# Another hand-written order on every engine, and 70 matmuls on a zero tile in the ramp

## The chip, the cores and the metric

One core of one Trainium2 chip. A core has TensorE (PE, with its weight loads shown as PEld), VectorE (DVE), ScalarE (ACT), GpSimd (POOL), SyncE (SP, which here only issues transfers) and 16 DMA engines. The metric is the device time of one execution in microseconds (us).

## The reference

Causal attention over q, k, v of shape (4 batches, 8 heads, 768 positions, 64), followed by a gated two-layer network over all 3072 rows:

```
scores = q @ k^T / 8
heads 0, 2, 6 (retrieval): keep keys at or before the query
heads 1, 3, 4, 5, 7 (stream): of these keep keys 0..3 and the last 64
a = softmax(scores);  x = a @ v, heads side by side: (3072, 512)
h = x @ w_in                 w_in (512, 2048)
g = h * sigmoid(beta * h)
out = g @ w_out              w_out (2048, 512), out in float32
```

## The kernel before

The work is cut into 8 chunks of 384 rows (half of a batch's positions; the first halves of batches 0 and 1 are chunks 0 and 1) and each chunk into 4 units of two heads. A unit's attention is: cast q and k to bf16, transpose them on PE, copy the transposes out of PSUM (`copy_qk`, L330 for k, L333 for q), multiply to scores (L451, `sp` banks), exp on ACT (L460), multiply with v (L520, `po` banks or a third kind, `mm`), divide by the sum on DVE (`normalize`, L529 and L533). Masks are added in PSUM by matmuls with an identity (L422) in the first 8 units, except unit 5; elsewhere DVE multiplies them onto the exps. Sink positions have copies of their own: `KO` for keys (L312), `VO` for v (L259, L260). Two units' results are transposed to `xT` (L558, copied at L567). From units 12 on q and k come as rows by GpSimd transfers (`load_rows`, L282) and are transposed by DMA.

The network follows per chunk: 16 groups of the first product (`steps_G1`, 4 matmuls of 128x384, L588), each with a tanh on ACT (L593) and a gate on DVE (L596); then, for each 128 rows, 4 groups of 4 matmuls of 128x512 of the second product (`steps_G2`, L641), a copy out on ACT (L645) and a store from SP.

There is no scheduler: each engine runs its instructions in the order in which the program emits them. That order is written out by hand, word by word. `RAMP` covers units 0 to 7 and the whole first product of chunks 0 and 1; `PLAN` has one line for each further unit; `TAIL` feeds what is left. `do` (L685 and after) reads a word: `ck`/`cq` cast k or q of a unit, the last letter being the engine (v DVE, a ACT, g POOL); `tk`/`tq` transpose, `kk`/`kq` copy the transpose out; `ad`, `qk`, `ex`, `ma` are the masks in PSUM, scores, exps and DVE masks of one tile of a unit; `pv` two of the six steps of the product with v; `no` normalize; `ko`, `vo` sink copies; `cv` cast a v tile; `lq`, `lv` load a chunk's q and k or a v tile by SP; `wi`, `wo` load a quarter of w_in or w_out by POOL; `ro` one transfer of rows by POOL; `xx`, `cx` transpose x and copy it out; `hm`, `hf` the first and second half of a first-product group, `mm`, `mA` a whole one (`mA` in an `sp` bank), `mb` a second-product group; `on` ones beside v; `ne`, `ml` masks; `be` beta; `tt` both transposes of a unit; `dk`, `dq` the DMA transposes of rows. In `PLAN`, `V` is a step of scores, `p` of the product with v, `a`/`A` and `b` groups of the two products, `T` and `X` transposes.

Ahead of the ramp, `idle(8, ps_m, "mm")` (L167) runs eight 128x512 matmuls on `zeros`, a bf16 tile of 128x512, while the first transfers are on their way.

PSUM has two `sp` tiles of two banks, three `mm` banks and one `po` bank. Stage tiles for q and k (`s0`, `s1`) and for v (`vs`) have two buffers each.

Of the kernel before, what the change touches and what calls it, by code (L numbers as in the profile page):

```python
# [10 lines left out]
F32 = mybir.dt.float32  # L11
# [7 lines left out]
def kernel(  # L19
# [13 lines left out]
    nc = tc.nc  # L33
    B, H, S, D = q.shape
# [467 lines left out]

    def steps_PV(u):
# [3 lines left out]
        def head(hh, qi, last):  # L507
            def go():
                for f in s["masks"] + chunk_values[u // NPAIR] if u >= 8 else []:
                    f()  # L510
                if "po" not in s:
                    if u < 8 and u % 2:
                        po = ps_m.tile([128, 512], F32, name="mm")
                        s["po"] = po[:, 0:HT * 2 * (D + 1)].rearrange("p (t h d) -> p t h d", t=HT, h=2)
                    else:
                        s["po"] = ps_o.tile([128, HT, 2, D + 1], F32, name="po")
# [168 lines left out]
    def do(word):  # L685
# [70 lines left out]
    def feed(x):  # L756
# [27 lines left out]
        mA mm ro3 mA mm ro3 mm mm ro3 mA mA mb mb tt8 mb mb mb
# [3 lines left out]
    for word in words:  # L788
# [27 lines left out]
        b a A p a p a a b a A p p A b a p b a p
        b A X a A b A
# [42 lines left out]
    i = 0  # L860
# [39 lines left out]
```

## Time and profile before

| | us |
|---|---|
| three runs | 228.45, 229.58, 230.4 (median 229.58) |
| the profiled execution | 231.07 |
| its span, first to last instruction | 229.1 |

The profile is of one execution. Spans and durations below are its own; the 1.97 us between the span and the execution's time lie around the span. A row of the timeline gives start, duration, engine (with a q for an issue by its queue), line, operation, output<-inputs, shape, count, and in brackets the idle time of that engine just before and what ended it.

### The profile page before, as it was taken

How to read it: one execution, taken by the hardware profiler on the slowest of the kernel's cores; microseconds unless marked ns; L12 is line 12 of the kernel's file. 1: busy time of each engine (PE TensorE's matmuls, PEld its weight loads, DVE VectorE, ACT ScalarE, POOL GpSimd, SP SyncE). 2: the span in 40 equal slices, each digit the busy share in tenths (PEclk: the TensorE clock that was granted, in tenths of full speed). 3: DMA queues.
4: the chain of work that ended last, by engine and by line, in shares of the span. 5: the costliest groups of instructions: out<-in, count | busy, mean ns of one | idle time of the engine just before them, and what ended most of it. 6: DMA issues, size and time to landing. Idle time of an engine off the chain costs nothing.

```text
span 229.1 us, 5018 instructions
## 1 busy us (share of the span) xinstructions
PE 223.1 (97%) x1907; PEld 127.4 (56%) x1907; DVE 141.8 (62%) x342; ACT 154.3 (67%) x254; POOL 87.6 (38%) x143
## 2 busy tenths in 40 slices
PE   7899999999999999999999999999999999999994
PEld 2456666654565665555654565455654656455553
DVE  4458988875286588536952588546963779028600
ACT  2567988864868799438944697759876878138621
POOL 5373991219636269535028038940560000000000
PEclk9999999999999999999999999999999999999999
DMA  6999999999999999969778969496983130111012
GB/s 202 262 297 247 215 197 203 232 193 161 196 142 97 181 164 156 122 173 156 111 149 109 158 132 173 86 163 93 194 70 83 47 83 0 49 46 46 0 49 92
DMA packets 95383, 31.66 MB, mean 138 GB/s; under 512 B 81776, under 2 KB 92416, under 8 KB 95360
## 3 DMA queue, kind: packets, MB, share of 16 engines
q1 hardware_dynamic: 58880, 22.82, 48.6%
q0 software_dynamic: 35904, 8.13, 39.8%
q10 hardware_dynamic: 576, 0.40, 0.5%
q8 instruction: 15, 0.25, 0.4%
q14 instruction: 8, 0.07, 0.1%
HBM read 27.27 MB, written 6.29 MB: 146 GB/s over the span
## 4 chain that ended last, share of the span: by engine, by line
PE 94%; DMA 2%; ACT 1%; SPq 0%; issue 0%; ACTq 0%
PE mm L641 35%; PE mm L588 25%; PE sp L588 12%; PE sp L451 8%; PE po L520 7%; PE mm L322 2%; DMA s<-in_k_dram 2%; PE sp L422 2%; PE mm L626 2%; PE mm L558 1%; PE mm L520 1%; PE mm L451 1%; ACT qkb L246 1%; SPq L119 0%; ACT es L460 0%; ACT KT L330 0%
## 5 line engine op out<-in xcount | busy, mean ns | idle before, releaser
L641 PE MATMUL mm<-w_out_sb,gT 128*128 128x512 bf16 x368 | 85.9, 379 | 0.0
L460 ACT ACTIVATE es<-sp 128x768 bf16<-128x768 f32 (+2 forms) x72 | 56.6, 837 | 21.4 <-PE sp L451 21.2
L588 PE MATMUL mm<-xT,w_in_sb 128*128 128x384 bf16 x348 | 64.6, 326 | 0.0
L588 PEld LDWEIGHTS <-w_in_sb 128*128 128x128 bf16 x512 | 47.8, 98 | 29.8 <-issue 0.2
L593 ACT ACTIVATE th<-mm,beta_h 128x384 f32<-128x384 f32 x87 | 49.7, 587 | 5.7 <-PE mm L588 0.9
L641 PEld LDWEIGHTS <-gT 128*128 128x128 bf16 x368 | 33.4, 98 | 36.0 <-issue 1.5
L596 DVE SCALAR_TENSOR_TENSOR gT<-th,mm 128x384 bf16<-128x384 f32 x87 | 46.7, 551 | 6.7 <-ACT th L593 3.2
L282 POOL DMA_DIRECT2D s<-in_q_dram x30 | 22.4, 763 | 26.3 <-DMA QTD<-s 19.8
L588 PE MATMUL sp<-xT,w_in_sb 128*128 128x384 bf16 x164 | 32.3, 326 | 0.0
L645 ACT ACTIVATE osb<-mm 128x512 f32<-128x512 f32 x23 | 13.9, 603 | 25.5 <-PE mm L641 25.2
L520 PEld LDWEIGHTS <-es 128*128 128x128 bf16 x472 | 23.8, 99 | 12.8 <-issue 1.5
L596 DVE SCALAR_TENSOR_TENSOR gT<-th,sp 128x384 bf16<-128x384 f32 x41 | 22.3, 552 | 5.6 <-ACT th L593 3.7
L282 POOL DMA_DIRECT2D s<-in_k_dram x30 | 22.4, 760 | 8.5 <-DMA w_out_sb<-in_moe_w_out_dram 5.8
L593 ACT ACTIVATE th<-sp,beta_h 128x384 f32<-128x384 f32 x41 | 23.7, 585 | 2.3 <-PE sp L588 0.2
L520 PE MATMUL po<-VX,es 128*128 128x65 bf16 x360 | 25.2, 195 | 0.0
L251 POOL CAST VX<-vs 128x512 bf16<-128x512 f32 x16 | 10.1, 632 | 36.4 <-DMA vs<-in_v_dram 30.2
L529 DVE RECIPROCAL rec<-po 128x6 f32<-128x6 f32 x28 | 5.4, 193 | 29.1 <-PE po L520 29.1
L451 PE MATMUL sp<-QTD,KT 64*128 64x128 bf16 (+2 forms) x258 | 20.1, 249 | 0.6 <-ACT QTD L333 0.4
L478 DVE TENSOR_TENSOR es<-es,Mh 128x768 bf16<-128x768 bf16 (+1 forms) x26 | 15.5, 626 | 5.0 <-ACT es L460 4.4
L533 DVE TENSOR_TENSOR x<-po,rec 128x384 bf16<-128x384 f32 x28 | 15.6, 557 | 1.0
L451 PEld LDWEIGHTS <-KT 64*128 64x128 bf16 x278 | 11.4, 96 | 6.2 <-issue 3.9
L259 POOL COPY VO<-VX 128x512 bf16<-128x512 bf16 x16 | 10.8, 696 | 6.2 <-DVE VX L251 6.2
(72 smaller groups left out, 160.3 us busy)
## 6 DMA issues: line engine op xcount, KB each, us to landing
vs<-in_v_dram SPq DMA_DIRECT2D x24, 256.0 KB, 5.2
out_dram<-osb SPq DMA_DIRECT2D x23, 256.0 KB, 2.6
w_in_sb<-in_moe_w_in_dram POOLq DMA_DIRECT2D x4, 512.0 KB, 9.3
w_out_sb<-in_moe_w_out_dram POOLq DMA_DIRECT2D x4, 512.0 KB, 16.8
s<-in_k_dram POOLq DMA_DIRECT2D x30, 64.0 KB, 4.8
s<-in_q_dram POOLq DMA_DIRECT2D x30, 64.0 KB, 4.9
s<-in_k_dram SPq DMA_DIRECT2D x4, 384.0 KB, 6.8
s<-in_q_dram SPq DMA_DIRECT2D x4, 384.0 KB, 6.5
```

The lines of the kernel that those rows point to most:

```text
L259: copy(out=vo[:, i - 1, :, 0:D], in_=vx[:, i, :, 0:D])
L282: nc.gpsimd.dma_start(out=ROWS[c % 2, name][:, t, i * 4 * D:(i + 1) * 4 * D].rearrange("p (h d) -> p h d", d=D), in_=src[b, i:H:2, r:r + 1 ...
L451: nc.tensor.matmul(sps[i][r][:, x * 128:y * 128], key(a, lhs), s["QT"][half(a), qi * 128:(qi + y - x) * 128], start=first, stop=first or y ...
L460: nc.scalar.activation(out=views[i].rearrange("p r k j -> p r (k j)"), in_=banks[2][:, :, 0:n * 128], func=ACTF.Exp, scale=scale)
L478: nc.vector.tensor_mul(ev[:, :, 0:n], ev[:, :, 0:n], Mh[h2][:, None, m0:m0 + n].to_broadcast([128, 2, n, 128]))
L520: nc.tensor.matmul(po[:, qi, hh, :], e, val, start=(j == 0), stop=(j == len(lst) - 1))
L533: nc.vector.tensor_mul(xg[g][:, :, :, u % 2, :].rearrange("p a t d -> p t a d"), po[:, :, :, 0:D], rec.to_broadcast([128, HT, 2, D]))
L588: nc.tensor.matmul(hp[:, 0:HALF], w_in_sb[:, mo, fi * 128:(fi + 1) * 128], xT[c][:, mo, :], start=(mo == 0), stop=(mo == MO - 1))
L593: nc.scalar.activation(out=th, in_=hp[:, 0:HALF], func=ACTF.Tanh, scale=beta_h[:, fi:fi + 1])
L596: nc.vector.scalar_tensor_tensor(out=gTs[c][:, fi, :], in0=th, scalar=1.0, in1=hp[:, 0:HALF], op0=ALU.add, op1=ALU.mult)
L641: nc.tensor.matmul(op, gTs[c][:, fi, ns * 128:(ns + 1) * 128], w_out_sb[:, fi, :], start=(fi == 0), stop=(fi == FO - 1))
L645: nc.scalar.activation(out=osb, in_=op, func=ACTF.Copy, scale=0.5)
```

## The change

`RAMP` and `PLAN` are replaced by another order of the same words, and one new word, `zz`. Beside it the words differ only in the engine of single steps (casts `ck`, `cq`, `cv`, copies `kk`, `kq` and `cx`, the ones `on`; among them cx0 goes from DVE to ACT and cx3 from ACT to DVE, the third v tile of chunk 0 from ACT to DVE, the key copies of units 0, 1 and 2 from DVE to ACT), in which loads POOL marks the buffer of first (a last letter `g` on `lq` and `lv`), and in a few first-product groups that are cut into halves or put into an `sp` bank. The word `zzN` issues N matmuls of a 128x122 slice of `zeros` into the columns 390 to 511 of the PSUM bank that holds unit 0's sums; these columns are read by nobody. The eight lots of 5, 5, 5, 15, 5, 15, 5 and 15 stand in the first three lines of `RAMP`. To make room for it, the `po` tile is now declared as a whole bank of 512 columns, of which the sums use the first 390.

On the engines' queues this gives, among much else: PE runs 10 zero matmuls right behind the eight wide ones, then unit 0's q and k transposes, then 25 more; POOL issues w_in's first quarter behind the sink copies `VO` of chunk 0 and the `KO` copies of units 1, 3 and 2, where before it stood ahead of `VO`; w_in's second quarter still stands behind the `KO` copies of units 6 and 5; ACT copies the transposed k of units 4 and 6 and the first x after the exps of unit 3. All weights are issued ahead of all rows in both orders. PE's real matmuls are the same 1907 less the eight on zeros; those of the first 8 units and of the first product of chunks 0 and 1 come ahead of the second product's first in both.

```diff
--- before.py
+++ after.py
@@ -500,6 +500,19 @@
         some = 3 if len(tiles) == 3 else 2
         return [visit(range(i, min(i + some, len(tiles)))) for i in range(0, len(tiles), some)]
 
+    banks_o = {}
+
+    def sums_bank(u):
+        if u not in banks_o:
+            banks_o[u] = ps_o.tile([128, 512], F32, name="po")
+        return banks_o[u]
+
+    def keep_busy(n):
+
+        z = HT * 2 * (D + 1)
+        for i in range(n):
+            nc.tensor.matmul(sums_bank(0)[:, z:512], zeros[:, 0:128], zeros[:, 0:512 - z], start=True, stop=True)
+
     def steps_PV(u):
         b, h2, p = units[u]
         s = st_u.setdefault(u, {})
@@ -513,7 +526,7 @@
                         po = ps_m.tile([128, 512], F32, name="mm")
                         s["po"] = po[:, 0:HT * 2 * (D + 1)].rearrange("p (t h d) -> p t h d", t=HT, h=2)
                     else:
-                        s["po"] = ps_o.tile([128, HT, 2, D + 1], F32, name="po")
+                        s["po"] = sums_bank(u)[:, 0:HT * 2 * (D + 1)].rearrange("p (t h d) -> p t h d", t=HT, h=2)
                 po = s["po"]
                 lst = s["blocks"][hh][qi]
                 for j, (e, val) in enumerate(lst):
@@ -744,6 +757,8 @@
             late[n].pop(0)()
         elif what == "tt":
             run(steps_T(n))
+        elif what == "zz":
+            keep_busy(n)
         elif what == "hm":
             opened.append(done[0])
             done[0] += 1
@@ -769,19 +784,17 @@
             wide[0] = False
 
     RAMP = """
-        ck0g ne1 lv0.0 lv0.1 tk0 ck2a ne0 cq0v ck1a tq0 kq0a ad0.0 on0v lv0.2 kk0v cq1v tq1 qk0.0
-        tk2 ad0.1 kq1v tk1 kk1v lq1.0g be qk0.1 ex0.0 ad1.0 cv0.0g ko1 lq1.1 ex0.1 pv0 ck3v cq3g tk3
-        lv1.0g cq2a tq2 kk3v lv1.1 cv0.1g ad1.1 qk1.1 kk2v ex1.1 tq3 ko2 qk1.0 wi0 vo0 cq4g lv1.2 cv0.2a
-        lq2.0g ko3 pv0 kq2v pv0 ad2.0 qk2.0 lv2.0 ex1.0 pv1 kq3a pv1 ck4v ad2.1 qk2.1 lv2.1 pv1 ex2.0
-        ad3.0 tq4 no0 tk4 ex2.1 ck7g kk4a qk3.0 ad3.1 qk3.1 no1 pv2 ck6v ex3.0 cq5v ck5g pv2 tk6
-        xx0 ad4.0 cq6g pv3 kq4v ex3.1 pv2 ad4.1 cx0v ad5.0 qk4.1 pv3 lv2.2 no2 on1g tq5 pv3 qk4.0
-        kk6a ml0 tk5 cq7g kq5v ex4.1 kk5a ko5 ko6 ad5.1 tq6 wi1 qk5.0 ex4.0 tk7 tq7 ex5.0 no3
-        qk5.1 ex5.1 kq6v xx1 ad6.0 kk7v wi2 kq7v wi3 cx1a qk6.0 ml1 ad6.1 ex6.0 cv1.1g ko7 qk6.1 cv1.0v
-        ex6.1 hm lq2.1 ma5.0 ma5.1 mm cv1.2g vo1 mm wo0 pv4 lv3.0g ad7.0 lv3.1 pv4 hf pv4 no4
-        qk7.0 ad7.1 pv5 pv5 ex7.0 lv3.2 qk7.1 pv5 no5 ml1 wo1 ex7.1 pv6 pv6 wo2 mm pv7 rq
-        pv7 pv7 no7 wo3 pv6 no6 rk cq8g xx2 ro3 cx2a mA mA ck8g xx3 cx3a mm mA
-        mm mA mm mm mA mm mm mm mA mm ro3 mm mm mA mm mm mm ro3
-        mA mm ro3 mA mm ro3 mm mm ro3 mA mA mb mb tt8 mb mb mb
+        lv0.0 cq0v on0g ck2a ck0g zz5 lv0.1 lv0.2 ne0 zz5 ck1v lq1.0 tq0 tk0 zz5 kk0a cq1g zz15 zz5 lq1.1g ne1 kq0v
+        ad0.0 ck3a be tq1 qk0.0 ad0.1 kq1v tk2 cq3v lv1.0g qk0.1 ex0.0 tk1 cv0.1v lv1.1 cv0.0g zz15 pv0 tk3 cq2g ex0.1
+        kk1a kk2a zz5 ad1.0 ad1.1 tq2 ko1 qk1.1 kk3v vo0 cv0.2v qk1.0 tq3 ko3 zz15 kq2v ex1.0 ko2 ck4v wi0 pv0 ad2.0
+        lv1.2 ad2.1 qk2.0 ex1.1 pv1 qk2.1 pv0 lq2.0 pv1 pv1 kq3a cq4g lv2.0 ml0 tq4 ex2.0 ad3.0 ex2.1 qk3.0 pv2 ck7g
+        cq7g no0 ad3.1 no1 qk3.1 ck6v tk4 ck5g tk6 lv2.1 cq5g xx0 kq4v ad4.0 ad4.1 ex3.0 ad5.0 pv2 pv2 ex3.1 pv3 cq6v
+        kk4a kk6a cx0a no2 pv3 qk4.1 tq5 ko6 pv3 rk kq5v ex4.1 tk5 qk4.0 no3 kk5a ad5.1 ex4.0 ko5 tq6 qk5.0 wi1 tk7
+        qk5.1 tq7 xx1 wi2 kq6v kk7v ad6.0 ex5.0 cv1.0g ex5.1 on1v ko7 qk6.0 ma5.0 lv2.2 cx1a ad6.1 ma5.1 lq2.1 ex6.0
+        qk6.1 hm wi3 pv4 cv1.1g hm cv1.2g lv3.0 ml1 ex6.1 hf vo1 mA kq7v pv4 wo0 pv5 hf ad7.0 pv4 no4 qk7.0 pv5 wo1
+        wo2 lv3.1 lv3.2 ex7.0 wo3 ad7.1 qk7.1 pv5 rq pv6 cq8g no5 pv6 pv6 ex7.1 hm pv7 hf ml1 pv7 pv7 xx2 cx2a mA no6
+        no7 ck8a mA xx3 cx3v mm mm mA mA mm ro3 mm mm mA mm mA mm mm mA mm mm mm ro3 mA mm mm mA mm ro3 mm mA mm mm mA
+        ro3 ro3 mb tt8 mb mb mb ro3
     """
     words = RAMP.split()
     on_vector = {int(w[2]) for w in words if w.startswith("ma")}
@@ -789,32 +802,32 @@
         do(word)
 
     PLAN = """
-        ro3 ro3 ck9v b cq9a dk3 b cv2.1v cv2.0v vo2 T ro3 cv2.2v V cq11v a ro3 ro3 ro3 ck11a ro4 a b
-        ck10a a dq3 a p cq10v a V p T p p p V p
-        b T b p p p p p V p
-        A b A a V ro4 p V a p p ro4 p p p
-        ro4 V b p p p b p p ro4 p V b
-        b p p p p X V p p a ro4 a ro4
-        b A ro4 a a p V p ro4 p p ro4 b ro4 a a A ro4 A b b b dk4 A V a p dq4 p b A b
-        p p p p p V p a a
-        p p A p V p p p
-        a a b b p p p p p p V a A A
-        a b p p p p V p p
-        b b a V p p p p p b a p
-        b A A a a A p a A A a p b a p A p p p A A V b b b A
-        p V p p p p p
-        a A a b b p p p V p p b p a A
-        a p A b p b p b A p b a p b p V A a
-        V a p p b p p b V p p A
-        b p p p p V p p
-        A a b V b b a a p p b p A p a p a a A A p b V a b A b b
-        p p p p V p p
-        a A V b p A A p p p V p p a A
-        a p b V b p p p p p
-        V b a p a p p V A p A b b p p A A a
-        p b V a p p p p A a p
-        b a A p a p a a b a A p p A b a p b a p
-        b A X a A b A
+        ck9a cv2.0v ro3 cq9g ro3 a ro3 dk3 ck11a cv2.1v V A T ro3 vo2 a cv2.2v b ro3 cq10v ro3 A ck10v cq11a b
+        ro4 a a a V p p T p V A p p dq3 p
+        T b A p ro4 p p p p p V b A
+        b V V a p p p p p p
+        V A p p p b p p V p a b ro4 ro4
+        p X p V p ro4 p p p b A a
+        A ro4 a p a ro4 V p p p b b a A ro4 A ro4 dk4 a p a V p b ro4 ro4 ro4 dq4 A A
+        p p a A p V p p p a b
+        p p A b V p p p p
+        b b p V p p p A p p
+        b a A b p p p p b b a p p V
+        b b a p p p p V p p a a
+        A A p a p b a p p A b A V b a p b b p b b A a
+        p A p p p V p p a
+        A b p a p b p b p p b V b p a a A
+        A a b A a a a p p p p a p V b p a
+        V b p p p p A p V a p b a
+        p V a p p p p A p
+        V b b a b A b p p a a p V b p p a a p A a A
+        b b p V p p p a p p b
+        V a b a p A p p p p V p
+        a b b p p V a p p p A p a b
+        V p p p b V b a b A p a a A p p b a A a A b
+        p b p p a p p p a V b A b
+        p p A p p b b p A p A
+        a A X A
     """.strip().split("\n")
     TAIL = "aaAaA"
```

## The prediction

> **What bounds the kernel now.** I read the page first, then busy time in stretches, then PE, ACT, POOL and the transfers in order of time up to 52 us.
>
> ```profile
> span 229.1 us, 5018 instructions
> PE 223.1 (97%) x1907; PEld 127.4 (56%) x1907; DVE 141.8 (62%) x342; ACT 154.3 (67%) x254; POOL 87.6 (38%) x143
> ...
> PE 94%; DMA 2%; ACT 1%; SPq 0%; issue 0%; ACTq 0%
> ```
>
> PE is busy for 223.1 of 229.1 us, and the chain that ended last is PE for 94% of its length. The stretches (us, then busy time and count of PE, PEld, DVE, ACT, POOL, the clock, the DMA share and GB/s) say where PE could still gain:
>
> ```profile
> 1.29:4.83 3.54, 3.54 (x8) 1.02 (x9) 1.38 (x5) 1.49 (x2) 2.61 (x10) 1.00 0.83 246
> 4.83:16.48 11.65, 10.44 (x89) 5.81 (x89) 6.24 (x17) 6.42 (x12) 5.98 (x16) 1.00 1.17 287
> 16.48:24.41 7.93, 7.69 (x109) 4.82 (x107) 7.02 (x17) 6.69 (x12) 3.82 (x10) 1.00 1.20 255
> 24.41:29.62 5.21, 5.21 (x76) 3.65 (x72) 5.14 (x11) 4.52 (x8) 5.15 (x10) 1.00 1.18 187
> 29.62:52.00 22.38, 22.38 (x150) 13.25 (x147) 18.71 (x37) 18.36 (x32) 7.72 (x12) 1.00 1.24 205
> 52.00:226.00 174.00, 173.84 (x1493) 98.82 (x1491) 102.94 (x258) 116.61 (x191) 61.67 (x85) 1.00 0.83 113
> 226.00:229.10 3.10, 0.00 (x0) 0.00 (x0) 0.00 (x0) 0.21 (x1) 0.00 (x0) 0.99 0.15 42
> ```
>
> From 24.41 to 226 us PE is full, 0.16 us apart. Its real matmuls are the same before and after, so what this order can win lies ahead of 24.41, and what it can lose is a hole that it tears later. Ahead of 24.41 PE is idle for 1.21 + 0.24 us, and it is slow. The clock column says 1.00 everywhere, but the durations contradict it (PE in order of time; start, duration, instruction):
>
> ```profile
> 1.29 3.59 PE L167 MATMUL mm<-zeros 128*128 128x512 bf16 x8 [1.29 <-DVE zeros L157]
> ...
> 16.48 0.83 PE L422 MATMUL sp<-Ns,idb 128*128 128x384 bf16 x2
> ...
> 26.11 0.49 PE L422 MATMUL sp<-Ns,idb 128*128 128x384 bf16 x2
> ...
> 31.41 0.51 PE L558 MATMUL mm<-idb,x 128*128 128x128 bf16 x6
> ```
>
> The same pair takes 0.83 us at 16.48 and 0.49 at 26.11, and the eight zero matmuls step by 3.54 / 8 = 0.44 us where the 128x512 stream at 50.88 (below) steps by 4.32 / 20 = 0.216. So PE ran at half speed until about 17 us. At half speed at most 10.44 / 2 = 5.2 us of the second stretch are surcharge.
>
> **The change part by part.** *The zero matmuls.* Not in the trace: 122 columns on 128 rows. From the steps above one costs 0.44 x 122/512 = 0.105 us slow or 0.216 x 122/512 = 0.051 us fast; 70 of them 7.4 or 3.6 us. By the order, ten follow the eight wide ones at once, and 25 more follow two lots of three transposes. So PE works without a gap from 1.29 through 4.83 + 10 x 0.105 = 5.9 and 0.6 of transposes to 6.5 and on to at least 6.5 + 25 x 0.051 = 7.8, at most 9.1. Before, PE was gapless only to 4.83, and the clock did not rise. I take it that the longer run raises it within this stretch and put the end of the 25 at 8.2. The Trainium skill ("TensorE: Matmul & The Clock Gate", Part 1) has the clock rise after one busy window of 3.4 us of a free-running grid, which would put it between 1.29 + 3.4 and 1.29 + 6.8 us here. The trace agrees that 3.54 us of work need not hold such a window. The same part says that the ramp penalty is under 1% of a typical span and should not be fitted: by that the change could win at most 2.3 us, by the rows up to 5.2.
>
> The lots of 15, 5 and 15 come later, when the first two exps are in work or done; fast, they cost 0.8 + 0.3 + 0.8 us, in PE time that is free because PE waits there for ACT and POOL (next). Without that cover they cost 1.9 us.
>
> *What the fast PE then waits for.* ACT in order of time (L460 are the exps, 512 or 768 wide; L333/L330 copies of transposed q and k; L567 a copy of transposed x):
>
> ```profile
> 8.18 0.81 ACT L460 ACTIVATE es<-sp 128x768 bf16<-128x768 f32 x1 [0.59 <-PE sp L451]
> 10.02 0.81 ACT L460 ACTIVATE es<-sp 128x768 bf16<-128x768 f32 x1 [1.03 <-PE sp L451]
> ...
> 12.58 0.60 ACT L460 ACTIVATE es<-sp 128x512 bf16<-128x512 f32 x1 [1.35 <-PE sp L451]
> ...
> 14.28 0.48 ACT L333 COPY QTD<-mm 128x384 bf16<-128x384 bf16 x1
> ...
> 18.18 1.31 ACT L460 ACTIVATE es<-sp 128x768 bf16<-128x768 f32 x2
> ...
> 21.66 2.01 ACT L460 ACTIVATE es<-sp 128x768 bf16<-128x768 f32 x3
> 23.53 0.83 ACT L567 COPY xT<-mm 128x768 bf16<-128x768 bf16 x1
> 24.21 1.57 ACT L460 ACTIVATE es<-sp 128x768 bf16<-128x768 f32 x2
> ...
> 27.56 1.36 ACT L460 ACTIVATE es<-sp 128x768 bf16<-128x768 f32 x2
> ```
>
> And POOL, with the transfers that matter (SP and POOL issues, then microseconds to landing of the same issue, from the DMA view of that moment), and three rows of DVE:
>
> ```profile
> 6.13 1.66 SPq L132 DMA_DIRECT2D vs<-in_v_dram  x1
> ...
> vs<-in_v_dram SPq DMA_DIRECT2D x1, 256.0 KB, 5.5
> ```
>
> ```profile
> 12.53 0.87 POOL L140 DMA_DIRECT2D w_in_sb<-in_moe_w_in_dram  x1
> 13.40 0.62 POOL L259 COPY VO<-VX 128x512 bf16<-128x512 bf16 x1
> 14.08 0.61 POOL L260 COPY VO<-VX 4x512 bf16<-4x512 bf16 x1
> 14.64 0.50 POOL L246 CAST qkb<-s 128x384 bf16<-128x384 f32 x1
> ...
> 15.16 0.28 POOL L312 COPY KO<-KT 128x128 bf16<-128x128 bf16 x1
> ```
>
> ```profile
> 12.14 0.55 DVE L333 COPY QTD<-mm 128x384 bf16<-128x384 bf16 x1
> ...
> 24.02 0.75 DVE L251 CAST VX<-vs 128x512 bf16<-128x512 f32 x1
> ...
> 30.79 0.56 DVE L533 TENSOR_TENSOR x<-po,rec 128x384 bf16<-128x384 f32 x1
> ```
>
> Walking the new queues with these durations:
> Unit 0's first scores stand behind the 25 zeros, two mask matmuls, beta's and a lot of three transposes (0.6 us): 8.8, and its exp starts at 9.1 instead of 8.18. The second follows at once, at 9.95 instead of 10.02. Then POOL decides: the last v tile of chunk 0 lands at 6.13 + 5.5 = 11.6, DVE casts it behind a key copy until 12.5, and POOL does VO 0.62, its sink rows 0.61, two KO 0.56, the issue of w_in's first quarter 0.87 and the cast of unit 4's q 0.50, until 15.8. PE's queue has that unit's transposes ahead of unit 3's masks and scores (0.2 + 0.3 + 0.3): unit 3's first exp starts at 16.7 instead of 18.18. This is 1.5 us won, whatever the clock did before 8 us. In it everything the POOL queue now holds behind sink values is counted: w_in's first quarter goes out at 14.4 instead of 12.53.
>
> From 16.7 ACT is full. Until the last exp of unit 6 it has six wide exps (6 x 0.81), two narrow (2 x 0.60), three key copies (3 x 0.48) and two x copies (2 x 0.83), together 9.16. The rows of two and three exps give back 0.05 to 0.1 at each handover (1.57 for 1.62, 2.01 for 2.22); twelve handovers give 0.8. So it ends at 16.7 + 8.35 = 25.1, with 0.2 for two waits 25.3; before it was 24.21 + 1.57 = 25.78. The new order put a key copy and an x copy, 1.3 us, behind unit 3 on ACT, where before one was done earlier and one by DVE; that eats most of the 1.5. Unit 7's two exps then follow three tanh as before: end 28.6 instead of 28.92. Units 6 and 7 are normalized by DVE back to back, and the transposes of xx3 wait for that in both orders (30.79 + 0.56, then 31.41). There the gain is 0.3 us.
>
> *The transfers as a second bound.* The last three issues of weights that PE needs, their times to landing, and the use (from the chain):
>
> ```profile
> 22.30 0.74 POOL L140 DMA_DIRECT2D w_in_sb<-in_moe_w_in_dram  x1
> ...
> w_in_sb<-in_moe_w_in_dram POOLq DMA_DIRECT2D x1, 512.0 KB, 7.3
> ```
>
> ```profile
> 29.96 0.77 POOL L144 DMA_DIRECT2D w_out_sb<-in_moe_w_out_dram  x1
> ...
> w_out_sb<-in_moe_w_out_dram POOLq DMA_DIRECT2D x1, 512.0 KB, 21.2
> ```
>
> ```profile
> 50.88 4.32 PE mm L641 x20
> ```
>
> w_in's second quarter lands at 29.6 and PE asks for it right behind xx2, at 29.62 + 0.3. w_out's last quarter lands at 51.2 and is asked for by the fourth group of the second product, at 50.88 + 0.86 = 51.74. The DMA share is over 1 in every stretch to 52 us. So even a PE that was ready much earlier would find a wall 0.54 us ahead of its present place, unless the queue itself starts earlier. In the new order w_in's second quarter stands behind the KO copies of units 6 and 5, so behind a key copy that I put at 20.7 to 21.1: issue at 21.5, 0.8 earlier. In front of it the first quarter is 1.9 us later (landing about 22.5 to 23, first use at 24). I book nothing for either.
>
> *The later order.* Counts are unchanged: 512 and 416 matmuls of the two products, all 128 of chunk 0 and 1 still stand ahead of the first of the second product. I book nothing for the new plan after 52 us; PE's 0.16 us there is the cover: any wait of another engine that reaches PE shows in full.
>
> Sum: -0.3 us on a span of 229.1, in an execution of 231.07 (1.97 lie around the span; 1.5 above the median). On the median: 229.58 - 0.3 = 229.3.
>
> **The rivals.** *The surcharge comes back (faster).* If v lands and POOL clears earlier than I walked, or ACT hands over faster, half the surcharge, 2.6 us, is won: 227.0. For it: 1.21 us of PE idle and 5.2 of slow time. Against it: the wall at 51.2, which must then also move by 2.1. Chance 0.20.
>
> *The software queue slips (slower).* One POOL queue carries all eight weight quarters between casts and copies. The first now goes out 1.9 us later. If the queue stays late by that, w_in's second quarter lands at 29.6 + 1.9 = 31.5 against a need at 29.6, w_out's last at 53.1 against 51.4, and the rows of the next chunks follow: with 0.5 to 0.9 more where the new plan meets late rows, 229.6 + 1.9 + 0.7 = 232.2. It decides once w_in's second quarter goes out after 22.6. Against it: the second issue depends on ACT, not on the first landing. Chance 0.14.
>
> *The clock stays down (the change does not do what it is for).* 3.54 us of zeros did not raise it at the start. If zeros never do, 70 slow ones cost 7.4 us, of which 1.2 fall into idle time: 229.6 + 6.2 = 235.8. Against it: PE's run without a gap is now over twice as long. Chance 0.07.
>
> **How the numbers follow.** A measurement of this kernel tells about 1% (2.3 us; the three runs lie 2 us apart) from no change. My forecast, no change that shows, has 0.59; faster by over 1% 0.20, slower 0.14 + 0.07 = 0.21. The likeliest case's own range is 228.0 to 231.0: 0.8 of earlier issue and 0.5 of slack below, waits of a microsecond or two above. To leave out no more than 2 in 10 it reaches to 227.0 and to 232.3; outside stay the clock that never rises and the further half of the faster case.
>
> **What would show it.** Right: the 128x384 pairs take 0.5 us before 12 us; ACT is full from about 16.7 to 25.3; xx3 at 31.1; PE without holes after. Wrong: a first exp of unit 3 before 15.5 or after 18, PE waiting for w_in_sb or w_out_sb, a hole over 1 us on PE after 31 us, or pairs at 0.83 us beyond 10 us.

## The result, and the profile after

| | median of 22 runs, us | range | ratio, 95% interval |
|---|---|---|---|
| before | 229.57 | 228.03 to 231.62 | |
| after | 230.46 | 229.85 to 231.95 | 1.0055 [1.0035, 1.0075] |

The change makes the kernel slower by half a per cent, 0.9 us, where 0.3 us less was forecast. (Ratios leave out runs more than 1.5% above the fastest of their kernel; medians take all.) Yet the profiled execution of the changed kernel, 230.47 us, has a span that is 0.4 us *shorter* than the one of before. The page of after:

```profile
span 228.7 us, 5130 instructions
PE 221.3 (97%) x1958; PEld 129.9 (57%) x1977; DVE 143.2 (63%) x340; ACT 154.7 (68%) x255; POOL 88.4 (39%) x141
...
PE 84%; DMA 7%; ACT 2%; SPq 2%; DVE 1%; issue 1%; ACTq 0%; POOL 0%; POOLq 0%
```

PE's share of the chain fell from 94 to 84% and transfers rose from 2 to 7%: something that PE waits for is now a DMA. First the ramp, PE in order of time (in after.py the lines stand 13 further down: L558 is L571, L588 L601):

```profile
11.19 0.71 PE L422 MATMUL sp<-Ns,idb 128*128 128x384 bf16 x4
...
23.20 0.50 PE L601 MATMUL mm<-xT,w_in_sb 128*128 128x384 bf16 x2
...
30.00 0.50 PE L571 MATMUL mm<-idb,x 128*128 128x128 bf16 x6
```

Four mask matmuls take 0.71 us at 11.19, where two took 0.83 at 16.48 before: the clock is up early, as forecast. The first use of w_in is at 23.20, where the walk put it at 24. The second lot of `xx` (the third of the page's x transposes; "xx3" below, as in the prediction) starts at 30.00, 1.4 us earlier than the 31.41 of before. So of the 1.4 us won by 30 us, 1.0 is lost again behind it: span minus the start of xx3 is 229.1 - 31.41 = 197.7 before and 228.7 - 30.00 = 198.7 after. I call that figure the rest; it splits ramp from plan in every profile. The work in it is the same: from xx3 on, the profile of before and a second one of after (e10 below) count 1623 matmuls each, of the same shapes in the same numbers. (The expectations' "loss behind the ramp", PE's time there beyond its usual spacing, is another measure of it: 2.4 us go with a rest of 197.7, 2.8 with 198.2.) Where it goes, PE's waits from 31 us on and the chain of waits in order of time (start, duration, what):

```profile
PE mm L601 <- DMA xT<-x: 0.4, 1, 0.4
```

```profile
147.13 0.56 DVE x L546
147.69 0.03 DVE es L492
147.72 7.47 DMA xT<-x
155.19 0.04 issue
```

PE waits 0.4 us for a transposing transfer of x that needs 7.47 us. Before, this view has no row for that stretch. (After has one more, 0.5 us of "issue" in three places ahead of second products; b2 below has it too, at a rest of 197.7, so it isn't the loss.) The view counts a wait only from the modelled end of the last matmul. The starts show more; PE in order of time, after:

```profile
132.31 1.46 PE L601 MATMUL mm<-xT,w_in_sb 128*128 128x384 bf16 x8
133.61 1.46 PE L601 MATMUL sp<-xT,w_in_sb 128*128 128x384 bf16 x8
135.16 1.46 PE L601 MATMUL mm<-xT,w_in_sb 128*128 128x384 bf16 x8
...
154.37 0.49 PE L601 MATMUL mm<-xT,w_in_sb 128*128 128x384 bf16 x2
155.23 1.14 PE L601 MATMUL mm<-xT,w_in_sb 128*128 128x384 bf16 x6 [0.37 <-DMA xT<-x]
```

Eight such matmuls step by 133.61 - 132.31 = 1.30 us, 0.163 each. The next eight need 135.16 - 133.61 = 1.55: 0.25 lost. The two ahead of the wait for x need 0.86 instead of 0.33: 0.53 lost. Together that is 0.8 of the 1.0.

### The profile page after: what moved, and what is told of

Read it like the earlier page. It is cut to its first block, busy times and chain, and to the rows that moved or that the text cites. A ratio compares the mean times of both kernels' runs of the same rounds, so it can differ in the third digit from the quotient of the medians.

```text
span 228.7 us, 5130 instructions
## 1 busy us (share of the span) xinstructions
PE 221.3 (97%) x1958; PEld 129.9 (57%) x1977; DVE 143.2 (63%) x340; ACT 154.7 (68%) x255; POOL 88.4 (39%) x141
## 4 chain that ended last, share of the span: by engine, by line
PE 84%; DMA 7%; ACT 2%; SPq 2%; DVE 1%; issue 1%; ACTq 0%; POOL 0%; POOLq 0%
PE mm L654 32%; PE mm L601 25%; PE sp L601 10%; PE sp L451 6%; PE po L533 6%; DMA s<-in_q_dram 4%; DMA xT<-x 3%; PE mm L639 2%; SPq L132 1%; ACT es L460 1%; PE mm L322 1%; PE mm L571 1%; PE sp L422 1%; PE mm L451 1%; SPq L119 1%
## 5 line engine op out<-in xcount | busy, mean ns | idle before, releaser
L654 PE MATMUL mm<-w_out_sb,gT 128*128 128x512 bf16 x349 | 84.1, 379 | 1.3 <-issue 0.5
L601 PE MATMUL mm<-xT,w_in_sb 128*128 128x384 bf16 x360 | 67.3, 326 | 0.5 <-DMA xT<-x 0.4
L460 ACT ACTIVATE es<-sp 128x768 bf16<-128x768 f32 (+1 forms) x72 | 56.4, 840 | 15.1 <-PE sp L451 15.1
L601 PEld LDWEIGHTS <-w_in_sb 128*128 128x128 bf16 x512 | 47.7, 98 | 30.8 <-issue 1.1
L609 DVE SCALAR_TENSOR_TENSOR gT<-th,mm 128x384 bf16<-128x384 f32 x90 | 48.5, 552 | 13.6 <-ACT th L606 9.8
L606 ACT ACTIVATE th<-mm,beta_h 128x384 f32<-128x384 f32 x90 | 51.4, 586 | 8.3 <-PE mm L601 3.6
L654 PEld LDWEIGHTS <-gT 128*128 128x128 bf16 x368 | 32.9, 98 | 34.7 <-issue 1.5
L601 PE MATMUL sp<-xT,w_in_sb 128*128 128x384 bf16 x152 | 30.0, 326 | 0.0
L533 PE MATMUL po<-VX,es 128*128 128x65 bf16 x360 | 25.3, 194 | 0.4 <-POOL VX L251 0.4
L606 ACT ACTIVATE th<-sp,beta_h 128x384 f32<-128x384 f32 x38 | 21.9, 583 | 3.5 <-PE sp L601 1.0
L609 DVE SCALAR_TENSOR_TENSOR gT<-th,sp 128x384 bf16<-128x384 f32 x38 | 20.5, 561 | 2.7 <-ACT th L606 0.7
L451 PE MATMUL sp<-QTD,KT 64*128 64x128 bf16 (+2 forms) x258 | 19.0, 240 | 0.1
```

What stands on the lines that cost most here:

```text
L451: nc.tensor.matmul(sps[i][r][:, x * 128:y * 128], key(a, lhs), s["QT"][half(a), qi * 128:(qi + y - x) * 128], start=first, stop=first or y ...
L460: nc.scalar.activation(out=views[i].rearrange("p r k j -> p r (k j)"), in_=banks[2][:, :, 0:n * 128], func=ACTF.Exp, scale=scale)
L533: nc.tensor.matmul(po[:, qi, hh, :], e, val, start=(j == 0), stop=(j == len(lst) - 1))
L601: nc.tensor.matmul(hp[:, 0:HALF], w_in_sb[:, mo, fi * 128:(fi + 1) * 128], xT[c][:, mo, :], start=(mo == 0), stop=(mo == MO - 1))
L606: nc.scalar.activation(out=th, in_=hp[:, 0:HALF], func=ACTF.Tanh, scale=beta_h[:, fi:fi + 1])
L609: nc.vector.scalar_tensor_tensor(out=gTs[c][:, fi, :], in0=th, scalar=1.0, in1=hp[:, 0:HALF], op0=ALU.add, op1=ALU.mult)
```

## The experiments

Four theories were stated after the first comparison. A: the profile of before shows an execution whose clock rose late; with an early clock the old ramp is at least as fast as the new one, and the new plan costs about 0.9 us. B: the new ramp always wins its 1.4 us and the plan costs 2.3. C: the ramp or its zeros cost time. D: PE is held by w_in's landing. All runs together (each against the kernel before on the same chip; b2 and e10 are single executions):

| run | ramp, plan | median, us | before | ratio, interval | xx3 | span | rest |
|---|---|---|---|---|---|---|---|
| first profile | old, old | 229.57 | | | 31.41 | 229.1 | 197.7 |
| b1 | old, old | 228.94 | 229.0 | 1.0006 [0.9971, 1.0041] | 31.23 | 228.9 | 197.7 |
| b2 | old, old | 228.61 | 229.24 | | 28.91 | 226.6 | 197.7 |
| after | new, new | 230.46 | 229.57 | 1.0055 [1.0035, 1.0075] | 30.00 | 228.7 | 198.7 |
| e10 | new, new | 230.03 | 229.38 | | 29.81 | 228.3 | 198.5 |
| e1 | new, old | 232.99 | 229.0 | 1.0161 [1.0111, 1.0211] | 30.01 | 231.4 | 201.4 |
| e2 | old, new | 231.05 | 229.0 | 1.0055 [1.0012, 1.0099] | 29.19 | 227.5 | 198.3 |
| e3 | new without zeros, new | 231.23 | 229.0 | 1.0079 [1.0046, 1.0111] | 30.49 | 229.5 | 199.0 |
| e4 | old with 40 zeros, old | 229.79 | 229.24 | 0.9999 [0.9964, 1.0033] | 28.62 | 228.1 | 199.5 |
| e5 | new, old (mended) | 229.62 | 229.24 | 1.0009 [0.9982, 1.0037] | 30.21 | 228.0 | 197.8 |
| e6 | new, new edited | 230.44 | 229.24 | 1.0051 [1.0021, 1.0081] | 29.94 | 228.1 | 198.2 |
| e7 | new, wide zeros; new | 229.76 | 229.38 | 1.0026 [0.9996, 1.0056] | 30.38 | 228.6 | 198.2 |
| e8 | new, wide zeros; old | 229.48 | 229.38 | 1.0028 [0.9995, 1.0060] | 29.33 | 227.3 | 198.0 |
| e9 | old, 4 wide zeros; old | 228.49 | 229.38 | 0.9974 [0.9942, 1.0006] | 29.30 | 227.0 | 197.7 |
| e11 | old, 6 wide zeros; old | 228.28 | 229.41 | 0.9963 [0.9928, 0.9998] | 28.94 | 226.6 | 197.7 |
| e12 | as e7, plan edited | 230.19 | 229.41 | 1.0031 [0.9998, 1.0064] | 29.61 | 228.8 | 199.2 |
| e13 | as e9 | 228.28 | 229.41 | 0.9972 [0.9934, 1.0009] | 28.63 | 226.3 | 197.7 |

### b1 and b2: the kernel before, twice more, unchanged

> The kernel before, profiled a second time. Theory A: the execution that was profiled first (231.07 us, 1.5 above the median) was one in which the PE clock rose late, at about 17 us; the moment differs from execution to execution, so the profiles of a kernel without long gapless PE work at the start differ. It expects a time near 229.5 and, where the profiled execution is near that, the last x transposes of chunk 1 (the second L558 lot after 29 us) at 30.0 to 30.6 us in place of 31.41, with 128x384 mask pairs already at 0.5 us before 16 us. Rival B: the ramp of before always ends at 31.4 us, and what differs between executions lies elsewhere (transfers, what lies around the span): L558 at 31.4 again whatever the time.

> The kernel before, a third profile, one look. Theory A: the moment at which the 128x384 pairs drop from 0.83 to 0.49 us, and with it the last x transposes of chunk 1, moves with the draw (31.41 and 31.23 us in the two slow draws so far); in a draw near 228.5 to 229 us they come at 29.0 to 30.2.

PE in order of time, b1:

```profile
7.75 0.34 PE L322 MATMUL mm<-idb,qkb 128*128 128x128 bf16 x3
8.15 0.41 PE L322 MATMUL mm<-idb,qkb 128*128 128x128 bf16 x3
...
11.70 0.50 PE L322 MATMUL mm<-idb,qkb 128*128 128x128 bf16 x3
...
15.46 0.49 PE L422 MATMUL sp<-Ns,idb 128*128 128x384 bf16 x2
...
29.92 1.47 PE L588 MATMUL sp<-xT,w_in_sb 128*128 128x384 bf16 x8 [1.27 <-DMA w_in_sb<-in_moe_w_in_dram]
31.23 0.50 PE L558 MATMUL mm<-idb,x 128*128 128x128 bf16 x6
```

And b2, the same rows:

```profile
9.00 0.50 PE L422 MATMUL sp<-Ns,idb 128*128 128x384 bf16 x2
...
28.91 0.50 PE L558 MATMUL mm<-idb,x 128*128 128x128 bf16 x6
```

Three transposes are 0.34 us fast and 0.50 slow. In b1 the clock is up at 7.75, falls during the next three, is down at 11.70 and up again at 15.46. In b2 it is up by 9.00 and stays. In the first profile it was down at 9.91 and 16.48. So the same program reaches xx3 anywhere between 28.91 and 31.41 us, with a rest of 197.7 each time, and in b2 it is 1.1 us *ahead* of the new ramp. In b1 PE also stood 1.27 us for w_in's second quarter: theory D's wait exists, but in the kernel before. (b1's profile was a late execution again, 230.82 us and xx3 at 31.23, where A had expected one near 229.5 and 30.0 to 30.6; b2's 28.91 is earlier than the 29.0 to 30.2 that A gave.)

### e1, e2, e3: one part of the change alone

e1 is the ramp of after with the plan of before (its first line shown), e2 the reverse, e3 is after without its zeros:

```diff
-        ck9a cv2.0v ro3 cq9g ro3 a ro3 dk3 ck11a cv2.1v V A T ro3 vo2 a cv2.2v b ro3 cq10v ro3 A ck10v cq11a b
+        ro3 ro3 ck9v b cq9a dk3 b cv2.1v cv2.0v vo2 T ro3 cv2.2v V cq11v a ro3 ro3 ro3 ck11a ro4 a b
...
-        lv0.0 cq0v on0g ck2a ck0g zz5 lv0.1 lv0.2 ne0 zz5 ck1v lq1.0 tq0 tk0 zz5 kk0a cq1g zz15 zz5 lq1.1g ne1 kq0v
+        lv0.0 cq0v on0g ck2a ck0g lv0.1 lv0.2 ne0 ck1v lq1.0 tq0 tk0 kk0a cq1g lq1.1g ne1 kq0v
...
```

> The new RAMP with its zero matmuls, and the PLAN of before. Theory A: the new ramp is worth nothing or little on the median of before, and the new plan is what costs the 0.9 us, through waits of PE between 130 and 165 us: 229.0 to 229.7, spread of the runs under 2 us. Rival B: the new ramp wins 1.4 us in every execution and the new plan loses 2.3: 228.2. Rival C (the new ramp itself costs the 0.9 us on the median): 230.5.

> The RAMP of before without zero matmuls, and the new PLAN. Theory A: 230.2 to 230.8, with the wide spread of before (3 us and more between runs). Rival B: 231.9. Rival C: 229.6, as before.

> The changed kernel with its eight lots of zero matmuls left out; nothing else differs. Theory A: the clock rises late and at a different moment in each execution, so the time is 231 to 232.5 with a spread of 2 us or more, and the 128x384 pairs take 0.83 us in a part of the ramp. Rival C (the zero matmuls themselves are what costs, about 0.9 us of PE time): 229.5. If the order alone sets the ramp through ACT and POOL and neither matters: 230.5, as with them.

e1 is no clean test: the new ramp has four second-product groups where the old has five, so the old plan runs one group out of step, and PE waits 1.3 and 0.9 us for exps (rest 201.4). e2, out of step the other way, shows a rest of 198.3 behind an old ramp. e3 says that the zeros help the new order: without them it is slower still (1.0079 against 1.0055, intervals overlapping, so not clear of noise). That speaks against theory C's zeros and leaves the plan.

### e4: 40 zeros in the old ramp

```diff
-        ck0g ne1 lv0.0 lv0.1 tk0 ck2a ne0 cq0v ck1a tq0 kq0a ad0.0 on0v lv0.2 kk0v cq1v tq1 qk0.0
+        ck0g ne1 lv0.0 lv0.1 tk0 zz3 ck2a ne0 cq0v ck1a tq0 kq0a ad0.0 zz7 on0v lv0.2 kk0v cq1v tq1 zz5 qk0.0
...
```

and `zz10`, `zz5`, `zz10` further on.

> The kernel before in its own order, with 40 zero matmuls in six lots (3 behind unit 0's k transposes, 7 behind its mask matmuls, 5 ahead of its first scores, 10, 5 and 10 ahead of the first products with v and of unit 1's scores) and nothing else. Theory A (the old ramp is at least as good as the new one as soon as the clock rises early in it; the new ramp only fixes the moment): the clock up by 9 us, the last x transposes of chunk 1 at 28.8 to 29.6 us, time 228.0 to 228.8 with a spread under 2 us, 0.3 to 0.6% faster than before. Rival C (zero matmuls cost what they occupy on PE): 229.5 to 231. Rival D (the second quarter of w_in holds PE whatever the clock does): L558 early, then a wait of PE for w_in_sb of about a microsecond, time as before.

xx3 came at 28.62, the earliest of all runs, and nothing was won: 229.79, ratio 0.9999. The chain of waits of e4 has the reason:

```profile
119.80 7.33 DMA xT<-x
127.13 0.04 issue
127.17 0.48 PE mm L601 x2
```

The transfer of x, 5.1 us in e13 from the same place, took 7.33, and PE stood 1.3 us, most of the 1.8 by which e4's rest of 199.5 exceeds 197.7. A's 228.0 to 228.8 was missed. The profiled execution (230.05) is one of six above 230; four of the twelve lie between 228.4 and 228.8, and whether this stall is what parts them isn't shown. Moving the ramp alone can move a stall into the dense part.

### e5 and e6: the plan

e5 is e1 with one more second-product group at the head of the old plan; e6 is after with two lines of its plan edited:

```diff
-        ro3 ro3 ck9v b cq9a dk3 b cv2.1v cv2.0v vo2 T ro3 cv2.2v V cq11v a ro3 ro3 ro3 ck11a ro4 a b
+        b ro3 ro3 ck9v b cq9a dk3 b cv2.1v cv2.0v vo2 T ro3 cv2.2v V cq11v a ro3 ro3 ro3 ck11a ro4 a b
...
-        A a b A a a a p p p p a p V b p a
+        A a p b p A p a p a a p a V b p a
...
-        V b b a b A b p p a a p V b p p a a p A a A
+        V b b b a A b p p a a p V b p p a a p A a A
```

> The new RAMP with the PLAN of before once more, now with one second-product group more at the head of PLAN, since the new ramp issues one fewer than the old one and the first trial left every later group of the plan one place late. Theory A: the PE waits of 0.9, 0.4 and 1.3 us between 139 and 170 us that the first trial had are gone, the loss after the ramp is 2.4 us as in the two profiles of before, and the time is 229.3 to 229.9 on a chip where before takes 229.6 (229.0 where it takes 229.0 or a little above). If the new ramp itself spoils the later stages (rival): 231 or more again.

> The changed kernel with two places of PLAN altered: in the line of unit 23 single steps of the product with v go between the first-product groups, where the trace has ten such groups in a row while DVE still multiplies masks (PE waited at 135 us); in the line of unit 26 a second-product group goes ahead of the first one that needs chunk 5's x (PE waited for the x transfer at 154.9 us). Theory A: these two waits are most of what the new plan costs beyond the old; 0.5 to 0.9 us less than the changed kernel: 229.6 to 230.0 where that takes 230.46. Rival: the waits move to other places, and the time stays within 0.2 us.

e5 is the clean form of e1. With the old plan the new ramp has a rest of 197.8 and a ratio of 1.0009 [0.9982, 1.0037]; with its own plan 198.7 and 1.0055. The new ramp alone is worth nothing that shows, and the plan costs about half a per cent. On one chip, e6, which differs from after by two lines of its plan, has a median of 230.44 against e5's 229.62. B falls: the new plan's price is 1 us, not 2.3. e6 removed the wait for x at 155 us (rest 198.2) and left the median where it was, at 230.44; its profile is its fastest execution, and what its other executions lost isn't known.

### e7 and e8: the zeros as fewer, wider matmuls

```diff
-        lv0.0 cq0v on0g ck2a ck0g zz5 lv0.1 lv0.2 ne0 zz5 ck1v lq1.0 tq0 tk0 zz5 kk0a cq1g zz15 zz5 lq1.1g ne1 kq0v
+        lv0.0 cq0v on0g ck2a ck0g zw1 lv0.1 lv0.2 ne0 zw1 ck1v lq1.0 tq0 tk0 zw1 kk0a cq1g zw5 lq1.1g ne1 kq0v
...
+        for i in range(n):
+            nc.tensor.matmul(sums_bank(0), zeros[:, 0:128], zeros, start=True, stop=True)
```

(`zw` is 512 columns wide; `zw3` replaces the 15 ahead of the first product of values. e8 is this ramp with e5's plan.)

> The changed kernel, but with its first six lots of zeros (50 matmuls on 122 columns, in five places) as 11 matmuls on 512 columns (1, 1, 1, 5 and 3), so about as much TensorE time with 39 fewer matmuls; the last two lots of 5 and 15 stay. Theory A (the 0.23 to 1.10 us for which TensorE waits near 15 us come from the 16 KB packets of the queue named instruction, which the many zero matmuls bring forward onto the transfer of chunk 1's q): the first such packet of the ramp comes after 13 us rather than at 10.3 to 11.8, chunk 1's q lands near 13.9 rather than 15.0, the wait at 15 us is gone, the second lot of xx starts at 29.0 to 29.6 rather than 30.0, and the kernel takes 229.6 to 230.0 us where the changed kernel took 230.44; what the new plan costs after 52 us stays. Rival (the wait at 15 us belongs to the new order of the ramp, GpSimd's cast above all): q lands when it lands, the wait stays above 0.2 us and the time within 0.2 us of the changed kernel's.

> The new ramp with the same wide zeros, and the plan of before (with one more second-product group at its head, as in the run with the new ramp and the old plan, 229.62 us). Theory A: that run less the 0.3 to 0.7 us of its wait at 15 us: 228.8 to 229.3 us, TensorE's loss behind the ramp 2.4 us as in every profile of the old plan, and the first run here that would be faster than the kernel before. Rival (the wait stays, or the old plan pays for the earlier ramp with a later transfer): 229.5 to 230.0 us.

> The changed kernel once more, one look. Theory A (its losses are properties of its order and its packets, not of one execution): the first packet of the queue named instruction in the ramp is at 10 to 11 us again, chunk 1's q lands near 15.0, TensorE waits 0.2 us or more near 15 us, and the transfer of x issued near 147.7 lands at 154.5 to 155.5 with a wait of TensorE behind it; the second lot of xx starts at 29.9 to 30.2. Rival (a draw): q lands below 14.2 or the waits at 15 and 155 us are gone, at a time within 0.5 us of 230.4.

Behind these stands a queue that no forecast of mine had in it. The DMA view from 10 to 12.5 us, e10 (after once more), then e7 (queue, packets, MB, share):

```profile
DMA packets 1144, 0.73 MB, mean 294 GB/s; under 512 B 296, under 2 KB 1143, under 8 KB 1143
...
q1 hardware_dynamic: 1143, 0.72, 110.4%
q8 instruction: 1, 0.02, 3.3%
```

```profile
DMA packets 1064, 0.67 MB, mean 269 GB/s; under 512 B 267, under 2 KB 1064, under 8 KB 1064
...
q1 hardware_dynamic: 1064, 0.67, 97.8%
```

One packet of 16 KB on the queue "instruction" falls into that stretch in e10 and in after, none in e7. The transfers of chunk 1's k and q that are in flight then take, from issue to landing, 5.9 us each in e10 and 4.9 in e7 (views of 6 to 8 and 8 to 10 us in e10, of 8 to 10 in e7):

```profile
s<-in_k_dram SPq DMA_DIRECT2D x1, 384.0 KB, 5.9
...
s<-in_q_dram SPq DMA_DIRECT2D x1, 384.0 KB, 5.9
```

```profile
s<-in_k_dram SPq DMA_DIRECT2D x1, 384.0 KB, 4.9
s<-in_q_dram SPq DMA_DIRECT2D x1, 384.0 KB, 4.9
```

All 17 profiles agree on this q. In the five with the 70 narrow zeros (after, e1, e5, e6, e10) the first packet starts at 10.2 to 11.8 us, and q takes 5.3 to 6.2 us. In the other twelve the first packet starts at 15.3 us or later, and q takes 4.9 to 5.1. A packet is short: e10's share of 3.3% of 16 engines in 2.5 us is 1.3 us on one engine, an estimate; q's delay is of that order. GpSimd casts q for unit 4, and PE waits for the cast. After, POOL in order of time:

```profile
11.67 0.62 POOL L259 COPY VO<-VX 128x512 bf16<-128x512 bf16 x1 [0.34 <-DVE VX L251]
...
13.47 0.88 POOL L140 DMA_DIRECT2D w_in_sb<-in_moe_w_in_dram  x1
15.14 0.50 POOL L246 CAST qkb<-s 128x384 bf16<-128x384 f32 x1 [0.79 <-DMA s<-in_q_dram]
```

PE, after and then e10:

```profile
15.70 0.34 PE L322 MATMUL mm<-idb,qkb 128*128 128x128 bf16 x3 [0.23 <-POOL qkb L246]
```

```profile
15.50 0.34 PE L322 MATMUL mm<-idb,qkb 128*128 128x128 bf16 x3 [0.84 <-POOL qkb L246]
```

In e1, e5 and e6 that wait is 0.29, 0.74 and 1.10 us. In e7 PE's waits between 9 and 16 us are gone, as theory A said, and e3, the new order without zeros, has no such wait either; the rival (it belongs to the new order) falls for that stretch. But xx3 came at 30.38, not at 29.0 to 29.6: PE now stood 0.5 us for w_in's second quarter, as in b1. e7 is nearer to the kernel before than after is (1.0026 against 1.0055, intervals overlapping). e10 repeats after's losses: a first packet in the same stretch, the 0.84 us wait, and a wait of 0.1 us for x at 154.7. e8 fell between the theories, 229.48; with the plans exchanged on the same ramp and chip e7 and e8 differ by 0.3 us in the median and not at all in the ratio, so the plan's price, plain in the rests, isn't confirmed by this pair.

### e9, e13, e11: a few wide zeros in the old ramp

```diff
-        ck0g ne1 lv0.0 lv0.1 tk0 ck2a ne0 cq0v ck1a tq0 kq0a ad0.0 on0v lv0.2 kk0v cq1v tq1 qk0.0
-        tk2 ad0.1 kq1v tk1 kk1v lq1.0g be qk0.1 ex0.0 ad1.0 cv0.0g ko1 lq1.1 ex0.1 pv0 ck3v cq3g tk3
+        ck0g ne1 lv0.0 lv0.1 tk0 ck2a ne0 cq0v ck1a tq0 kq0a ad0.0 zw1 on0v lv0.2 kk0v cq1v tq1 zw1 qk0.0
+        tk2 ad0.1 kq1v tk1 kk1v lq1.0g be qk0.1 ex0.0 ad1.0 cv0.0g ko1 lq1.1 ex0.1 zw2 pv0 ck3v cq3g tk3
```

e13 is e9 again; e11 has one more `zw1` behind `tk0` and `zw2` behind `ad0.0`.

> The kernel before with four zero matmuls on 512 columns (one behind the mask of unit 0's first step, one ahead of its first scores, two ahead of its first first-product of values) and nothing else changed. Theory A (the old ramp is good once the clock rises early; the price of the 40 narrow zeros was a packet of the queue named instruction that fell on a transfer of x at 120 us): the clock rises before 7 us, the second lot of xx starts at 28.6 to 29.0, the packets stay within 1 us of where the kernel before has them, and the time is 228.5 to 229.0 us with a narrow spread. Rival (the moment of the rise does not follow four matmuls): the rise stays spread between 5 and 17 us and the time is that of the kernel before, 229.0 to 229.6 us.

> The kernel before with its four wide zero matmuls once more (228.49 us against 229.38 for the kernel before on that chip, ratio 0.9974 with an interval that just takes in 1). Theory A: 228.3 to 228.9 us, a ratio of 0.995 to 0.999, second lot of xx at 28.7 to 29.4 us. Rival (that gain was chance): a ratio of 0.999 to 1.003.

> The kernel before with six zero matmuls on 512 columns in the ramp (one behind the first transposes of k, two behind the mask of unit 0, one ahead of its first scores, two ahead of its first product of values); nothing is left out. Theory A (the time of the kernel before is spread because the moment of the clock's rise is, and a gapless run of TensorE from 1.3 to about 7.5 us fixes that moment): the clock rises before 7.5 us, the second lot of xx starts at 28.6 to 29.1, all runs lie within 1.2 us of the fastest, the median is 228.1 to 228.6 us and the ratio's interval lies below 1. Rival (the spread of the kernel before has other causes, transfers or packets that fall differently): the spread stays 2 to 3 us as with the kernel before, and the median is within 0.4 us of it.

e13's page and its PE in order of time:

```profile
span 226.3 us, 5026 instructions
```

```profile
8.85 0.50 PE L422 MATMUL sp<-Ns,idb 128*128 128x384 bf16 x2
...
28.63 0.50 PE L576 MATMUL mm<-idb,x 128*128 128x128 bf16 x6
```

Four to six matmuls more, and the old ramp keeps its early clock in all three profiles: xx3 at 29.30, 28.63 and 28.94, rest 197.7. e11 is faster than the kernel before with an interval just below 1; the intervals of e9 and e13, one kernel run twice, take 1 in. All three medians lie 0.9 to 1.1 us below that of the kernel before on their chips. e11's expectation of a spread of 1.2 us was missed: nine of twelve runs lie within 0.8 us of 227.99, two at 229.48 and one at 233.04. So the clock is not the only thing that varies.

### e12: the plan at 135 us

```diff
-        A b p a p b p b p p b V b p a a A
-        A a b A a a a p p p p a p V b p a
+        A b p a p b p b p b V b p a p a A
+        A p a p b A p a a p a p a V b p a
```

> The changed kernel with the wide zeros, and two lines of its plan (those of units 22 and 23) edited so that no more than three groups of first products follow one another without a first product of values between them; in the profiles of the new plan five such groups stand in a row at 132 to 136 us, where VectorE's gates come late. Theory A (that place costs 0.4 us of TensorE's time, the price of the new plan that every profile of it shows): the wait for the gate at 135 us goes, TensorE's loss behind the ramp falls from 2.82 to 2.4 to 2.5 us, and the median from 229.76 to 229.3 to 229.5 us. Rival (VectorE is late there whatever stands between, and its lateness moves to the next group): a wait of 0.1 us or more stays between 130 and 145 us, loss behind the ramp 2.7 us or more, same median as with the wide zeros alone.

PE's waits from 31 us on, e7 and then e12:

```profile
PE mm L606 <- DVE gT L614: 0.2, 1, 0.2
```

```profile
PE sp L606 <- DMA xT<-x: 1.0, 1, 1.0
```

The wait for the gate went from the view, and the time did not fall. By the starts, eight matmuls took 135.55 - 133.93 = 1.62 us at that place in e7 and take 135.85 - 134.35 = 1.50 in e12, where 1.30 is usual: the loss shrank from 0.3 to 0.2. The rest is 199.2, of which 1.0 in the view, and 1.2 by the starts, is a wait for x at 126.7 that lies ahead of the edit. Neither theory holds whole.

## Why the prediction was wrong

**The failed step is "I book nothing for the new plan after 52 us".** It cost 0.8 to 1.0 us: a rest of 198.5 and 198.7 in the two profiles of after against 197.7 in six of the seven profiles of the old ramp with the old plan (the seventh, e4, holds the stall shown above) and 197.8 in e5. By the starts of PE's matmuls two places make up most of it: the wait for x at 155 us, 0.53 in after and 0.27 in e10, and the place near 135 us, 0.25 and 0.32, where the view of e10 and e7 names a gate of DVE. Some 0.2 is not attributed, and why the transfer of x is slow there stays open. The prediction had named the cover, PE's 0.16 us, and what a wait would do; it then left a plan of 26 rewritten lines at zero because the counts were equal.

**The second step that failed is the carrying over: "-0.3 us on a span of 229.1 ... On the median".** It noted that the profiled execution lay 1.5 us above the median and took the gain off the median all the same. That excess sits in the very stretch that the change rewrites: xx3 at 31.41 there, at 28.91 in b2. An estimate from the profiles: with 197.7 behind it and 1.9 to 2.0 around the span (231.07 - 229.1, 228.61 - 226.6), the median of 229.57 puts xx3 at about 29.9 in a usual execution; after's 230.46 less 198.6 and 1.7 to 1.8 puts it at about 30.1. So on the median the new ramp won nothing, as e5 says too, and the plan's loss is the result. The spans of single executions bear it out: the 229.1 of the first profile is near the upper end of the kernel before, 226.0 to 230.3 with a median of 227.5 in 29 executions on another chip, while after's 228.7 is the median of its 22. That the two profiles differ by -0.4 us, close to the forecast of -0.3, is luck: 1.4 won and 1.0 lost, neither of them foreseen.

**The steps of the ramp.** Against the execution that it was made on the walk was too timid: -1.4 us, not -0.3.
- The zeros raise the clock early: right. But the eight zeros of before, 3.54 us, can raise it by themselves: in b1 the transposes at 4.84 already took 0.34 us. They don't keep it up: there it was down again by 9.14, where two mask matmuls took 0.82.
- Unit 3's first exp at 16.7: measured 16.67, by two errors that cancel. POOL was 0.8 to 0.9 us ahead of the walk (v arrived in time: VO at 11.67 instead of 12.5, w_in's issue at 13.47 instead of 14.4), and then waited 0.79 us for q's transfer, which the walk didn't contain. Part of that wait is the price of the zeros, booked as free in PE's idle time: without the early packet POOL waited 0.34 us there in e3 and 0.33 in e7, and PE not at all for that cast.
- ACT behind it: the last exp of unit 6 was to end at 25.3 and ended at 24.53, unit 7's at 27.75 instead of 28.6, ACT in order of time:

```profile
16.67 1.30 ACT L460 ACTIVATE es<-sp 128x768 bf16<-128x768 f32 x2 [0.63 <-PE sp L451]
...
22.92 1.61 ACT L460 ACTIVATE es<-sp 128x768 bf16<-128x768 f32 x2
...
26.45 1.30 ACT L460 ACTIVATE es<-sp 128x768 bf16<-128x768 f32 x2 [0.26 <-PE sp L451]
```

From 16.67 to 24.53 are 7.86 us for the 13 instructions to which I gave 8.6: they overlap by more than the 0.8 booked. xx3 follows: 30.00 instead of 31.1.
- w_in's second quarter as a wall: right as a mechanism. It stopped PE in b1 (1.27 us) and e7 (0.5), not in after's profile, where it went out at 20.82 instead of 21.5. The wall of w_out's last quarter at 51.2 moves with the ramp: in b2 it went out at 27.55 and landed 20.5 us later, at 48.1, with no change of order.
- Two readings in the working are off and enter no sum: the DMA share is 0.83, not over 1, in the first stretch, and w_out's need stands once as 51.74 and once as 51.4.

**The rivals.** "The surcharge comes back" was half true and belonged to the kernel before: b2 has it back without any change. "The software queue slips" did not occur in the two profiles of after, and the clock that stays down did not either. That the transfer of q would be late in the ramp, or one of x a hundred us behind it, was no rival in the prediction, and should have been.

## What to carry to other kernels

Where a profile lies above the median, find where the excess sits before a gain is carried over: here it sat in the stretch to be changed, and two more profiles of the unchanged kernel showed it (the first alone, b1, would not have). Split a span at one landmark that both kernels pass, and compare the two parts; a plan that is rewritten can cost something even at equal counts. Measure a wait from start to start, too: the view showed 0.4 us where 0.8 were lost. If spare matmuls are to keep TensorE busy, few wide ones are the safer choice here: 70 narrow ones brought an instruction packet onto a transfer that PE waits for, four to six wide ones did not.

## What the hardware showed

*The clock.* The same program had its clock up for good by 9 us, up and down and up by 15.5, or up only after 16.5 us. The spans of these executions differ by up to 2.5 us of 226.6 (1.1%) with the same rest of 197.7; 1.27 of it is, in b1, the wait for w_in. The Trainium skill ("TensorE: Matmul & The Clock Gate", Part 1) calls the window free-running and the start of the fast clock variable from run to run, with which the traces agree; it puts the penalty under 1% of a typical span, and here the difference between two executions is already more.

*Instructions are traffic.* The page's queue q8 moves 15 packets and 0.25 MB, 16 KB each, and their times follow TensorE's instruction count: the first starts at 17.0 to 18.8 us in the eight profiles with at most six matmuls added, at 15.3 to 16.1 in the four with 31 or 40 and at 10.2 to 11.8 in the five with 70. That the packets are TensorE's instructions is inferred from that, from nothing else. The Trainium skill ("Runtime: NRT & Kernel Launch", Instruction fetch mechanics) has each engine's sequencer fetch blocks of 16 KiB, 256 instructions, by a DMA queue of its own, at a cost that is mostly hidden. The size agrees; the cost isn't hidden here, since q took 5.3 to 6.2 us instead of 4.9 to 5.1 and PE waited 0.23 to 1.10. For the transfers of x in the dense part the link is not shown: from 119 to 150 us they took 4.7 to 7.5 us with a packet in flight and 3.7 to 6.9 without one, and one of before, issued at 162.6, took 7.4 without one.
